# Strided v, band k and the xT ring of an attention-plus-feed-forward kernel: longer load runs with on-chip copies, and one tile fewer per ring

## The chip, the cores and the metric

The kernel runs on one core of a Trainium2 chip. The time is the device time of one launch in microseconds, as the median of several runs; most runs of the kernel before agree within some 0.3%. A run over 1.5% above the fastest of its kernel counts as slow and stays out of the ratios. HBM is the memory from which the loads read, SBUF the core's own memory, and PSUM, in banks, what matmuls write. Engine names in the profile: PE is TensorE's matmuls, PEld its weight loads, DVE VectorE, ACT ScalarE, POOL GpSimd, SP SyncE. The program fixes the order of each engine's instructions, and an engine that waits for one stands with all that come behind it, as PE will be seen to for 7.3 us; that matters more here than anything else.

## The reference, cut to what matters

```python
# q, k, v: 8 batches x 8 heads x 576 tokens x 64, fp32 in HBM
scores = (1 / sqrt(64)) * q @ k.T
mask_local   = (rel >= 0) & (rel < 32)              # heads 0..3: a band
mask_strided = (rel >= 0) & (pos_k % 32 == pos_q % 32)   # heads 4..7
attn = softmax(where(mask, scores, -1e9)) @ v
x = attn.transpose(0, 2, 1, 3).reshape(4608, 512)
h = maximum(x @ w_in, 0)                            # 512 -> 2048
out = (s * (h * h) + b) @ w_out                     # 2048 -> 512
```

The feed-forward part is called F1 (x @ w_in) and F2 (@ w_out). The loads turn fp32 into fp16, so a run that this text gives in bytes of an fp16 tile is twice as long in HBM. Attention is done in pairs of heads, four pairs to a batch (0 and 1 in the band, 2 and 3 strided), and its small matmuls are interleaved with those of F1 and F2.

## The kernel before: the parts that the change and the argument touch

The order of instructions isn't written by hand. While the program is built, a `Plan` keeps a clock for each engine, takes the next matmul step that its clock calls ready, and puts each helper copy on the engine on which it would end first by listed prices. The engines afterwards execute what came out, in that order, whatever the real times are.

```python
def flush(self):
    ...
    eng = min(p[1], key=lambda e: max(self.free[e], r) + p[1][e])
    end = max(self.free[eng], r) + p[1][eng]
    self.free[eng] = end
    p[2](eng)
```

The copy that pairs the heads of q or k (96 x 768, into a tile called qp or kp; batches 0 and 1 do without it) may go to ACT, to DVE or, in batches 1 to 3, to POOL. The issue of a whole batch's loads is also POOL's work:

```python
plan.post([key], {"A": 810, "V": 350, **({"P": 900.0} if b in (1, 2, 3) else {})}, g, ...)
...
plan.post(..., {"P": 0.0}, lambda eng, b=b: fetch_qk(b + 2), [("fetch", b + 2)])
plan.post([("fetch", b + 2)] + both("vs", b), {"P": 0.0}, lambda eng: fetch_v(b + 2), ...)
```

A third copy, the spread of a transposed q, may also go to POOL at a price of 2000, in late batches. The attention output (kind "a") of batch 0 takes its PSUM banks in rotation from a list:

```python
if b == 0:
    banks = {"a": [f2, f2, f1], "t": [t, a], "s": [("s", SB), ("s", SB), f1]}[kind]
```

Strided v of batches 0 to 3 comes as one load per batch (`vs`, 1 KB rows) and is copied on chip into `v_str`, of which there are two; batches 4 to 7 come as four loads straight into `v_str`, in short runs of one row of 64 elements (256 bytes in HBM), because `v_str` has a column of ones behind each row:

```python
def load_vs(b):
    vs = v_str[b % NV]
    for h in range(4):
        nc.gpsimd.dma_start(out=vs[:, h, :, 0:D],
                            in_=v[b, 4 + h].rearrange("(p j) d -> p j d", j=ST))
```

The softmax here doesn't subtract the row's maximum and nothing guards it: scores larger than these inputs give would overflow.

## Time and profile before

| before | value | how to read it |
|---|---|---|
| median time | 312.08 us | of 3 runs, 311.35 to 312.26; 311.72 in the 4 runs beside the changed kernel |
| span of the profiled run | 309.0 us | the profile's own clock; the launch time is about 2 us more |
| PE / DVE / ACT / POOL busy | 97% / 71% / 58% / 32% | a busy PE can hide waits; the others are far from full |
| packets of the software queue | 57,200 | the loads that POOL issues |

Two rows of slices, each a fortieth of the span (7.7 us), digits in tenths: POOL and the clock granted to PE.

```profile
POOL 8562559934951592059202950000000000000000
PEclk9999999999999999999999999999999999999999
```

POOL has work until about 185 us. The clock is full everywhere.

### The profile page before, as it was taken

What the parts mean: (1) busy time and instruction counts of PE and PEld (TensorE: products, weight loads), DVE (VectorE), ACT (ScalarE), POOL (GpSimd) and SP (SyncE); (2) the same over time, 40 slices, a digit from 0 to 9 for tenths busy, and PEclk for the clock granted to TensorE, in tenths of its full rate; (3) what the DMA queues carried; (4) which work ended last, traced back from release to release, by engine and by line L of the source; (5) the groups of instructions that cost most, each with busy time, mean ns of one, the idle gap of its engine ahead of it and who ended that gap; (6) DMA issues with size and microseconds to landing.
All of it is one profiled execution on the core that took longest, in us unless ns stands there. A gap on an engine that the chain in (4) does not pass through costs nothing.

```text
span 309.0 us, 6715 instructions
## 1 busy us (share of the span) xinstructions
PE 300.5 (97%) x2526; PEld 194.4 (63%) x2526; DVE 218.2 (71%) x575; ACT 178.3 (58%) x336; POOL 99.8 (32%) x146
## 2 busy tenths in 40 slices
PE   8899999989999999999999999999999999999994
PEld 3765655555656655556687755565677666766883
DVE  7567958799976877859755874589866366737653
ACT  1876945769736964668055736694945445356300
POOL 8562559934951592059202950000000000000000
PEclk9999999999999999999999999999999999999999
DMA  7999999998999699679998999842010100200313
GB/s 127 204 212 205 216 175 159 219 135 122 99 165 176 86 147 155 110 110 183 150 174 153 128 146 159 172 92 88 2 36 34 68 2 34 104 1 0 105 67 106
DMA packets 99940, 37.28 MB, mean 121 GB/s; under 512 B 81170, under 2 KB 95890, under 8 KB 99906
## 3 DMA queue, kind: packets, MB, share of 16 engines
q0 software_dynamic: 57200, 18.08, 60.9%
q1 hardware_dynamic: 42706, 18.76, 29.9%
q8 instruction: 20, 0.33, 0.5%
q14 instruction: 14, 0.11, 0.1%
HBM read 36.84 MB, written 10.32 MB: 153 GB/s over the span
## 4 chain that ended last, share of the span: by engine, by line
PE 82%; DMA 9%; DVE 4%; issue 2%; ACT 1%; POOL 1%; SPq 0%; DVEq 0%; POOLq 0%; ACTq 0%
PE ps_f L877 35%; PE ps_f L926 20%; PE ps_f L845 12%; DMA ql<-in_q_dram 6%; PE ps_s L531 4%; PE ps_a L585 2%; DMA w_out_sb<-in_v_dram 2%; PE ps_s L845 2%; PE ps_t L585 1%; PE ps_t L845 1%; PE ps_s L926 1%; PE ps_t L411 1%; DMA out_dram<-o 1%; PE ps_t L633 1%; DVE gT L908 1%
## 5 line engine op out<-in xcount | busy, mean ns | idle before, releaser
L877 PE MATMUL ps_f<-xT,w_in_sb 128*128 128x512 f16 (+1 forms) x632 | 148.0, 357 | 0.0
L899 ACT ACTIVATE u<-ps_f 128x512 f16<-128x512 f32 x137 | 81.1, 596 | 72.8 <-PE ps_f L877 69.5
L877 PEld LDWEIGHTS <-w_in_sb 128*128 128x128 f16 x640 | 68.1, 113 | 34.5
L926 PE MATMUL ps_f<-w_out_sb,gT 128*128 128x512 f16 x304 | 80.7, 379 | 0.2 <-DVE gT L908 0.2
L908 DVE TENSOR_TENSOR gT<-u 128x512 f16<-128x512 f16 x111 | 48.1, 438 | 31.7 <-ACT u L899 30.6
L926 PEld LDWEIGHTS <-gT 128*128 128x128 f16 x320 | 28.9, 98 | 23.2 <-DVE gT L908 0.5
L845 PEld LDWEIGHTS <-gT 128*128 128x128 f16 x320 | 31.0, 98 | 8.7
L845 PE MATMUL ps_f<-w_out_sb,gT 128*128 128x256 f16 x184 | 25.9, 273 | 0.0
L611 DVE TENSOR_TENSOR x_nat<-ps_a,rec 72x256 f16<-72x256 f32 (+1 forms) x52 | 23.7, 456 | 0.6
L547 ACT ACTIVATE p_loc<-ps_s 128x384 f16<-128x384 f32 x46 | 21.1, 493 | 5.1 <-PE ps_s L531 4.8
L547 ACT ACTIVATE p_str<-ps_s 72x432 f16<-72x432 f32 (+1 forms) x46 | 21.0, 485 | 3.2 <-PE ps_s L531 2.9
L585 PEld LDWEIGHTS <-p_str 72*128 72x128 f16 x256 | 15.5, 98 | 11.2 <-issue 1.4
L906 ACT ACTIVATE gT<-u 128x512 f16<-128x512 f16 x33 | 20.8, 630 | 1.0
L293 POOL DMA_DIRECT2D v_loc<-in_v_dram x28 | 20.6, 764 | 1.8 <-DVE qD_loc L315 1.8
L937 DVE SCALAR_TENSOR_TENSOR o<-ps_f,s_sb,bcs 128x512 f32<-128x512 f32 x19 | 14.1, 747 | 9.4 <-PE ps_f L926 9.2
L298 POOL DMA_DIRECT2D v_str<-in_v_dram x16 | 13.0, 815 | 10.7 <-PE ps_a L585 3.7
L555 DVE TENSOR_TENSOR p_str<-p_str,mask_str 72x432 f16<-72x432 f16 (+1 forms) x42 | 14.7, 360 | 1.3 <-ACT p_str L547 1.0
L555 DVE TENSOR_TENSOR p_loc<-p_loc,mask_loc 128x384 f16<-128x384 f16 x42 | 14.6, 360 | 1.2 <-ACT p_loc L547 0.9
L845 PEld LDWEIGHTS <-S 128*128 128x128 f16 x128 | 12.5, 98 | 3.2
L315 ACT COPY xT<-ps_t 128x576 f16<-128x576 f16 x9 | 5.7, 637 | 13.4 <-PE ps_t L633 13.4
L600 DVE RECIPROCAL rec<-ps_a 72x4 f32<-72x4 f32 (+1 forms) x52 | 9.1, 176 | 6.1 <-PE ps_a L585 5.5
L585 PEld LDWEIGHTS <-p_loc 128*128 128x128 f16 x192 | 10.1, 98 | 5.2 <-issue 0.7
(158 smaller groups left out, 406.4 us busy)
## 6 DMA issues: line engine op xcount, KB each, us to landing
out_dram<-o SPq DMA_DIRECT2D x34, 256.0 KB, 3.1
w_out_sb<-in_moe_w_out_dram POOLq DMA_DIRECT2D x4, 512.0 KB, 11.1
v_loc<-in_v_dram POOLq DMA_DIRECT2D x28, 72.0 KB, 7.8
ql<-in_q_dram POOLq DMA_DIRECT2D x6, 288.0 KB, 6.4
qs<-in_q_dram POOLq DMA_DIRECT2D x6, 288.0 KB, 6.2
ks<-in_k_dram POOLq DMA_DIRECT2D x6, 288.0 KB, 7.6
kl<-in_k_dram POOLq DMA_DIRECT2D x4, 288.0 KB, 8.9
kl<-in_k_dram POOLq DMA_DIRECT2D x16, 72.0 KB, 3.9
```

Source lines behind the costliest of these rows:

```text
L293: nc.gpsimd.dma_start(out=vl[LPAD:128, h, :, 0:D], in_=v_band(b, h))
L547: nc.scalar.activation(out=pt[0:nk, 0:2 * n].rearrange("k t c -> k (t c)"), in_=st["s", g][0:nk, 0:2 * n * nq], func=AF.Exp, scale=scale)
L555: nc.vector.tensor_tensor(out=pt[0:nk, 0:2 * n], in0=pt[0:nk, 0:2 * n], in1=mask, op=ALU.mult)
L585: nc.tensor.matmul(out=st["a"][:, j % per, :], lhsT=st["pw", g][0:nk, i * nq:i * nq + WIDE], rhs=vt[0:nk, 2 * mm + e, j, :])
L611: nc.vector.tensor_tensor(out=st["x"][:, j0:j0 + per, 64 * e:64 * e + 64], in0=st["pa", e, j][0:nq, 0:per, 0:D], in1=st["rec", e, j][0:nq, ...
L845: nc.tensor.matmul(out=gts[name, T, t][:, 0] if halves else gts[name, T][:, t], lhsT=lhs(k, t), rhs=rhs(k), start=fresh and k == 0 and (ha ...
L877: nc.tensor.matmul(out=gts["h", T, ft][:, lo:hi], lhsT=w_in_sb[min(ft // 4, 2)][:, ct].rearrange("p (c x l) -> p c l x", x=128, l=4)[:, ma ...
L899: nc.scalar.activation(out=gts["u", T, ft], in_=gts["h", T, ft], func=AF.Relu)
L906: nc.scalar.activation(out=gts[T][:, ft, :], in_=u, func=AF.Square)
L908: nc.vector.tensor_tensor(out=gts[T][:, ft, :], in0=u, in1=u, op=ALU.mult)
L926: nc.tensor.matmul(out=gts[id_], lhsT=gts[T][:, ft, ts * 128:(ts + 1) * 128], rhs=w_out_sb[:, ft, cols], start=(ft == 0), stop=(ft == NFT ...
L937: nc.vector.scalar_tensor_tensor(out=o[:, 0:n], in0=gts[id_], scalar=s_sb[:, 0:1], in1=bcs[:, cols], op0=ALU.mult, op1=ALU.add)
```

## The change

Its intent: fewer and longer runs in HBM. Strided v of all batches is loaded in 1 KB rows (2 KB in HBM) and copied on chip; k of the band heads of batches 4 to 7 is loaded in 768-byte runs (1.5 KB in HBM), paired by a copy, transposed by DMA and spread by another copy. SBUF for this is won by a single `v_str`, a single `vs`, and a ring of three instead of four batches in xT. The core of the diff:

```diff
-    v_str = [const.tile([SQ, 4, ST, D + 1], FP16, name=f"v_str{i}") for i in range(NV)]
+    v_str = const.tile([SQ, 4, ST, D + 1], FP16)
...
-    NX = 4
+    NX = 3
...
-            if b >= (QB_DMA if name == "q" else KB_DMA):
+            if name == "q" and b >= QB_DMA:
...
-    def load_vs(b):            # (four loads a batch, removed with its use for b >= 4)
...
-        plan.post([key], {"A": 810, "V": 350, **({"P": 900.0} if b in (1, 2, 3) else {})}, g,
+        plan.post([key], {"A": 810, "V": 350, **({"P": 900.0} if b in (1, 2, 3) or name == "k" else {})}, g,
...
+        free = [("a", (b - 1, 2 + mm), 1, ST - 1)] if b and not loc else []
-        plan.post([key], {"P": 1000.0} if loc else {"A": 2 * (170 + 0.83 * n), "V": 540.0}, g,
+        plan.post([key] + free, {"P": 1000.0} if loc else {"A": 2 * (170 + 0.83 * n), "V": 890.0}, g,
...
-            banks = {"a": [f2, f2, f1], "t": [t, a], "s": [("s", SB), ("s", SB), f1]}[kind]
+            banks = {"a": [f2, f2, f1 if m < 3 else a], "t": [t, a], "s": [("s", SB), ("s", SB), f1]}[kind]
...
+        def k_spread(eng):
+            st["k"] = kT_loc[mm]
+            copy_on(eng, out=st["k"][:, LPAD:LPAD + S].rearrange("d (p j) -> d p j", j=nt),
+                    in_=loaded[b, "kTl"][:, mm].rearrange("d j p -> d p j"))
+        if k_by_dma and loc:
+            plan.post([("in", "kl", b, mm)], {"D": 1300.0}, k_dma, [("kTl", id_)])
+            plan.post([("kTl", id_), ("s", (b - 1, m), 2)], {"V": 757.0, "A": 660.0}, k_spread, [("k", id_)])
...
-        loaded[b, "vs"] = inp.tile([SQ, NS], FP16, tag="vs", name="vs")
+        loaded[b, "vs"] = inp.tile([SQ, NS], FP16, tag="vs", bufs=1, name="vs")
```

Cut: the pair buffers go from 3 to 5, some tiles change pools, and one latency that the plan assumes for DMA transposes before 110 us goes from 5.5 to 12 us. The line on `banks` concerns one attention pair of batch 0. The changed kernel needs it: without it the plan, with its single `v_str`, stops with no step left that could become ready.

## The prediction

> **What bounds the kernel now.** I began with the page, to see which engine is full and what the chain that ended last consists of.
>
> ```profile
> PE 300.5 (97%) x2526; PEld 194.4 (63%) x2526; DVE 218.2 (71%) x575; ACT 178.3 (58%) x336; POOL 99.8 (32%) x146
> ...
> PE   8899999989999999999999999999999999999994
> ...
> DMA  7999999998999699679998999842010100200313
> ...
> q0 software_dynamic: 57200, 18.08, 60.9%
> ...
> PE 82%; DMA 9%; DVE 4%; issue 2%; ACT 1%; POOL 1%; SPq 0%; DVEq 0%; POOLq 0%; ACTq 0%
> ```
>
> The DMA row is nearly full to about 210 us, which makes it look like a transfer problem. But 82% of the chain is PE. A busy PE can hide waits, so I took the time per matmul from the chain, where runs of one kind follow each other without a gap:
>
> ```profile
> 146.48 3.02 PE ps_f L926 x14
> ...
> 236.53 4.04 PE ps_f L845 x37
> ```
>
> 3.02/14 is 0.216 us for a matmul of 512 columns, 4.04/37 is 0.109 for 256. In the same way the chain gives 0.083 for 192 columns, 0.063 for 144, 0.055 for 128, 0.043 for 96, 0.033 for 65 and 72, and 0.023 and 0.063 for two kinds that run beside each other (paired transposes of the first batches, sums over w_out). Multiplied by the counts of the program, in its order, this is the PE stream: 293.6 us in all, of which 5.1 are filler matmuls of the start. The last matmul ends near 304.5, then an eviction and a store take the rest of the 309.0 us. So PE stands still for about 11 us, and where is decisive. The first transpose of batch 1's q starts at 29.10 us, at 21.9 us of the stream: 7.2 us of the idle time lie before it, in the start, which waits for first loads. From 29.10 to 304.5 the clock advances 275.4 us and the stream 271.65, so only 3.75 us are left there. The chain shows most of those in one place:
>
> ```profile
> 60.45 0.19 DVE rec L600
> 60.65 1.65 DVE v_str L315 x4
> 62.30 0.46 DVE x_nat L611
> 62.76 0.06 DVE gT L908
> 62.82 0.78 issue
> ```
>
> That is four copies of strided v in a row on DVE, holding back an attention eviction. The table by stretches says how full the helpers are there and later (columns: stretch, length, then busy us and instructions of PE, PEld, DVE, ACT, POOL, then clock, DMA share, GB/s):
>
> ```profile
> 95.00:210.00 115.00, 115.00 (x919) 71.80 (x918) 82.62 (x252) 72.90 (x141) 40.79 (x61) 1.00 1.33 142
> 57.00:77.00 20.00, 18.74 (x177) 11.27 (x175) 18.57 (x43) 16.66 (x33) 10.54 (x16) 1.00 1.07 165
> ```
>
> DVE is 93% busy from 57 to 77 us, but 72% from 95 to 210, with ACT at 63%. After 95 us the chain is PE alone: late batches, which this change is about, keep no PE waiting. The waits seen there belong to others:
>
> ```profile
> ACT u L899 <- PE ps_f L877: 69.5, 77, 6.7
> POOL gate L997 <- DMA kT<-ks: 35.0, 6, 16.4
> ```
>
> ACT stood idle 69.5 us for matmuls, and POOL 35.0 for a transpose before loading a batch two ahead; both are slack.
>
> **What the Trainium skill says.** "Perfetto Trace Analysis", section "Identifying the Most-Contended Engine": matmul busy time doesn't show how near the limit a kernel is, since matmuls are pipelined. The trace agrees: busy counts 379 ns for a matmul that advances the chain by 216, hence the stream above. "DMA: Bandwidth & Descriptors", section "Why small descriptors are slow (HBM only)": each packet of a short HBM transfer pays a fixed overhead, 27% for one of 256 bytes. That is the length of the source runs which the change replaces. The trace fits without proving it: the software queue moves 18.08 MB in 60.9% of the engines' time, and the hardware queue 18.76 MB in 29.9%. "SBUF — State Buffer", section "Who interferes with whom": VectorE and GpSimd share a pair of ports, and a VectorE instruction with two SBUF inputs contends with a GpSimd one that reads SBUF. The trace agrees: of these two rows the second has gT products at 0.8 us each, where their median is about 0.41:
>
> ```profile
> 72.11 3.03 POOL L315 COPY qD_str<-qT 64x576 f16<-64x576 f16 x4 [7.76 <-DMA qT<-qs]
> 72.27 1.59 DVE L908 TENSOR_TENSOR gT<-u 128x512 f16<-128x512 f16 x2
> ```
>
> **The change part by part.** *Strided v, batches 4 to 7.* A batch's four loads of 72x8 runs become one of 72x4: 2304 runs to 288. Issues on POOL: 12 fewer at 0.81 us, 9.8 us. Added are 16 copies of 72x512, at 0.29 to 0.40 us on DVE or 0.62 on ACT. In the built program the copies rise from 6 to 20 on ACT and from 10 to 12 on DVE: 14x0.62 = 8.7 us of ACT, 0.8 of DVE. DVE's share in the crowded early stretch falls, because the plan prices a pair at 890 instead of 540. v_str becomes single, so a batch's copy also waits for the previous batch's last use.
>
> *Band k, batches 4 to 7.* 2304 runs to 384 a batch; 12 fewer issues at 0.75 us, 9.0 us of POOL. Added: 8 pairing copies (in the build 2 more on ACT at 0.83, 2 on DVE at 0.35, 4 on POOL at 0.93) and 8 spreads of 128x576: 5 on ACT at about 0.64, 3 on DVE at perhaps 0.4. The DMA transposes stay 8. Together with v, ACT gains 13.6 us in the late stretch (63% to 75%), DVE about 3 (72% to 75%), and 4x0.93 of POOL copies disturb DVE less than their own length. POOL loses some 19 us of issuing. About 15,700 runs leave the software queue of 57,200 packets. All of it lies beside PE: value on the path, 0.
>
> *Ring of three.* xT of batch b may be written one F1 tile or more later. In both built orders I compared the last reader's place with the next need: for batch 6 the write is free at 169 us of the stream and F1 of tile 6 begins at 204; for batch 7 it is free at 200, needed at 230. A transpose of x lands in 9.3 us, so nothing waits. The wrap cuts two tiles instead of one, 64 matmuls more, with the same columns: 0.1 us.
>
> *The order that results.* The change also alters planned latencies, so the whole order is made anew. Stream after: 294.4 us, of which 5.8 filler. Up to q of batch 1 it has the same length (21.95), but 0.7 of useful work was displaced by filler; what is left behind 29.1 us is 272.4, +0.8. Next, in before 6 F1 matmuls (1.3 us) stand between transposes of q and k of batch 1, and PE still waited a little for k at 31.15; after has 3 (0.65), with k's and q's strided transposes directly behind one another. Those loads do not land sooner, so PE should wait 0.7 us for k and some 0.2 for strided q: +0.9. In exchange part of the jam at 60 to 66 us goes: -0.6. For copies on ACT or DVE that now and then stand ahead of an eviction in order, I allow +0.4.
>
> Sum: 0.8 + 0.9 - 0.6 + 0.4 = +1.5. The launch time follows the span, so 312.1 + 1.5, rounded down a little because late waits may absorb some of the start's: 313.4 us.
>
> **The rivals.** *The transfers are the limit after all*, and short runs cost several per cent: for it, the full DMA row; against it, the chain after 95 us and ACT's wait for PE. It would give 300 to 306. *DVE and ACT become the bound*: copies of 1.2 us in pairs on ACT ahead of the relu that frees one of two F1 banks. For it: F1's four matmuls take only 0.86 us. Against: 75% load, and the plan interleaves F2 and attention. It would cost 0.3 us a time, up to 5 in all: 316 to 319. *The longer path of k* (load, pairing, transpose, spread) comes late and PE stalls in order: against it, the plan allows 12 us for a transpose that lands in 2.8 to 9.3; for it, two copies sit on POOL behind a wait for another transpose. One late batch costs 2 to 5 us: 315 to 318. *A pure gain at the crowded stretch*, with no waits in the start: 310.
>
> **Range and chances.** The path offers at most 3.75 us behind the start, so faster by 2% (under 305.8) needs the start to shrink as well, and its loads are unchanged: 0.02. Slower by 2% (over 318.3) needs two rivals at once, or one badly: 0.07. Within 2%: 0.91. Eight in ten: 310.5 to 316.8.
>
> **What would show it.** Right: packets of the software queue near 41,000 and its share well below 60.9%; POOL busy near 85; ACT near 190; chain after 95 us still PE; the first q transpose still near 29.1, and a wait for k of batch 1 just behind it; the four-in-a-row v copies gone from the chain. Wrong: v_str, kT_loc or kTl named as releasers of PE for over 1 us in sum after 95 us; PE waiting for xT; a PE gap in late slices; or an end below 308, which would mean that transfers did hold PE in a way this chain doesn't show.

## The result, and the profile after

The changed kernel took 325.85 us (median of 4 runs, 323.69 to 329.22) beside 311.72 for the kernel before (4 runs, 311.12 to 312.26). It is slower by 4.3%: the ratio is 1.043, with an interval of 1.034 to 1.053. Ratios here are the mean time of one kernel's fast runs over that of the other's from the same rounds, so not quite the ratio of the medians quoted. One of the four runs, 329.22, counted as slow and is left out of it. The three fast ones still lie 4 us apart, where those of the kernel before lie within 1.1; why is not known. All runs gave right results.

The page of the changed kernel: busy times, the rows of slices, the software queue and the chain that ended last.

```profile
PE 305.3 (95%) x2593; PEld 199.3 (62%) x2593; DVE 223.6 (69%) x586; ACT 189.5 (59%) x351; POOL 83.6 (26%) x122
...
PE   8898994699999999999999999999999999999995
...
PEclk9999799599999999999999999999999999999999
...
q0 software_dynamic: 38384, 18.07, 46.7%
...
PE 77%; DMA 11%; POOL 4%; issue 3%; DVE 2%; SPq 1%; ACT 1%; POOLq 0%; DVEq 0%; ACTq 0%
```

The loads did what they were meant to: a third fewer packets, their share of the DMA engines down from 60.9% to 46.7% for the same 18 MB (58.6 to 62.5% in the four traces with 57,200 packets, 46.7 to 53.5% in the eight with 38,384). The time is lost elsewhere, and the PE row says where: the seventh and eighth digits, 4 and 6, are a hole of some 7 us around 55 us. The clock row has a 5 right behind it, and a 7 near 36 us. That is in batches 1 and 2, whose loads the change leaves as they were.

I read the waits next (columns: engine and line, what it waited for; us in total, times, the longest).

```profile
POOL vs L288 <- ACT v_str L308: 26.4, 3, 10.7
...
PE ps_t L405 <- POOL qp L308: 7.3, 1, 7.3
```

PE waited once, for 7.3 us, for qp, the paired q of batch 2, copied by POOL. The other line, POOL's 26.4 us for the copies into `v_str` before it may issue a load of `vs`, becomes important later. Here is PE around the hole, with start, length, engine, line, operation and, in brackets, what it waited for:

```profile
51.23 0.40 PE L954 MATMUL ps_s<-w_out_sb,w_mix 128*32 128x512 f16 x4
58.93 0.66 PE L405 MATMUL ps_t<-ident,qp 96*128 96x96 f16 x6 [7.30 <-POOL qp L308]
```

And POOL in the same stretch of the changed kernel. The first line issues the strided v of batch 2; the six behind it load q and k of batch 3, for which no step of batch 2 needs to wait:

```profile
50.33 0.73 POOL L288 DMA_DIRECT2D vs<-in_v_dram  x1 [0.21 <-issue]
51.06 0.67 POOL L273 DMA_DIRECT2D ql<-in_q_dram  x1
51.72 0.67 POOL L273 DMA_DIRECT2D kl<-in_k_dram  x1
52.38 1.80 POOL L282 MEMSET qs<- 16x2048 f16 x1
54.48 0.72 POOL L288 DMA_DIRECT2D qs<-in_q_dram  x1 [0.30 <-POOL qs L282]
55.19 1.80 POOL L282 MEMSET ks<- 16x2048 f16 x1
57.28 0.72 POOL L288 DMA_DIRECT2D ks<-in_k_dram  x1 [0.30 <-POOL ks L282]
58.05 0.82 POOL L308 COPY qp<-ql 96x768 f16<-96x768 f16 x1
```

Without a gap to speak of, five issues of about 0.7 us and two memsets of 1.80 us stand ahead of the copy. The data had landed long before: ACT copied the other pair of the same tile at 50.5 us. The plan had none of these issues on its clock: it charges 0 for them. The surprise is in the kernel before, where POOL did the same thing at nearly the same time. First POOL's copy of a batch 2 pair there, then the transposes of PE that use it, then DVE's copy of the other pair:

```profile
57.31 0.82 POOL L315 COPY qp<-ql 96x768 f16<-96x768 f16 x1
```

```profile
58.47 0.41 PE L411 MATMUL ps_t<-ident,qp 96*128 96x96 f16 x6
```

```profile
48.26 0.31 DVE L315 COPY qp<-ql 96x768 f16<-96x768 f16 x1
```

In both kernels one qp copy of batch 2 lands on POOL at the end of this burst. Before, it was that of the *second* pair, done at 58.13, and PE asked for it at 58.47, so it was in time by 0.34 us; the first pair's had been done by DVE at 48.57. In the changed kernel POOL has the *first* pair's, which PE wants as soon as the matmuls placed ahead of it are done, at 51.63. The changed order did not make POOL slower; it gave POOL's late slot to an operand that is needed some 7 us sooner.

The table by stretches shows the cost behind the wait too (stretch, length, then busy us and instructions of PE, PEld, DVE, ACT and POOL; then granted clock, DMA share, GB/s). After:

```profile
32.00:36.00 4.00, 3.51 (x47) 2.80 (x47) 2.17 (x5) 2.92 (x6) 3.05 (x5) 0.59 1.15 218
...
51.00:59.00 8.00, 0.70 (x11) 0.34 (x10) 0.78 (x3) 0.95 (x2) 7.36 (x9) 0.85 1.53 168
59.00:64.00 5.00, 5.00 (x37) 2.95 (x38) 1.49 (x6) 1.61 (x3) 3.53 (x5) 0.56 1.39 139
```

Before:

```profile
51.00:59.00 8.00, 8.00 (x84) 4.86 (x83) 5.97 (x16) 4.00 (x8) 7.36 (x9) 1.00 1.33 179
59.00:64.00 5.00, 4.72 (x46) 2.75 (x45) 4.61 (x12) 3.79 (x8) 5.00 (x7) 1.00 1.39 227
```

POOL is busy 7.36 us of the 8 in both; PE is busy 8.00 in one and 0.70 in the other. From 59 to 64 us PE is busy all the time, yet executes 37 matmuls at a clock of 0.56. The Trainium skill, "TensorE: Matmul & The Clock Gate", section "What's actually happening", says that the clock halves after at least one idle window of about 3.4 us and comes back after a busy one. The traces agree in length: the slow stretches of the changed kernel last 3.4 us (32.7 to 36.1) and 6.8 us (56.6 to 63.4), one window and two. They don't agree that the window before must be wholly idle; the last section comes back to this. In a slow stretch a matmul takes about twice as long, so the first one costs 1.7 us, and the second, in which PE stood until 58.93, about 2 us.

**The account.** As in the prediction, I multiplied the matmul durations by the counts of the program to get the time for which PE's stream needs a full clock, and took the rest as standing still, or as slow clock. (A wait counted in this way, between the starts of matmuls, comes out 0.1 to 0.2 us longer than in the brackets above, which count from the end that the profile models.) For the start of the last matmul:

| term | before | after | difference |
|---|---|---|---|
| PE's stream at full clock | 293.87 | 294.70 | +0.83 |
| standing, 0 to 15 us | 4.05 | 4.03 | 0.0 |
| standing, 15 to 45 us (first loads, q and k of batch 1) | 2.73 | 4.45 | +1.7 |
| standing, 45 to 60 us (qp of batch 2) | 0.70 | 7.63 | +6.9 |
| standing, 60 to 90 us (the jam on DVE) | 1.98 | 0.85 | -1.1 |
| standing, after 90 us | 0.05 | 1.79 | +1.7 |
| half clock | 0 | 3.57 | +3.6 |
| start of the last matmul | 304.4 | 318.1 | +13.7 |

Each column is about 1 us short of its last row, because the first matmul starts at 1.05 or 1.07 us. The differences add up within rounding to 13.6. The spans of these two traces differ by 12.9 us, since what follows the last matmul is 0.8 us shorter in the changed kernel. The largest single wait after 90 us is one of 0.72 us that ends at 152.1. POOL's timeline ahead of it, and PE's matmuls behind it:

```profile
141.76 2.89 POOL L270 DMA_DIRECT2D ql<-in_q_dram  x4 [0.31 <-issue]
...
149.73 0.73 POOL L288 DMA_DIRECT2D vs<-in_v_dram  x1
150.46 1.56 POOL L308 COPY qD_str<-qT 64x576 f16<-64x576 f16 x2
...
152.07 0.35 PE ps_s L530 x3
```

It is the same pattern: POOL issues the loads of a late batch from 141.76 to 150.46 us, and the spread of a q that PE soon stands for comes behind them.

### The profile page after: what moved, and what is told of

Same layout as the page of the kernel before. It is cut to its first block, busy times and chain, and to the rows that moved or that the text cites.

```text
span 321.9 us, 6836 instructions
## 1 busy us (share of the span) xinstructions
PE 305.3 (95%) x2593; PEld 199.3 (62%) x2593; DVE 223.6 (69%) x586; ACT 189.5 (59%) x351; POOL 83.6 (26%) x122
## 3 DMA queue, kind: packets, MB, share of 16 engines
q0 software_dynamic: 38384, 18.07, 46.7%
## 4 chain that ended last, share of the span: by engine, by line
PE 77%; DMA 11%; POOL 4%; issue 3%; DVE 2%; SPq 1%; ACT 1%; POOLq 0%; DVEq 0%; ACTq 0%
PE ps_f L878 32%; PE ps_f L927 19%; PE ps_f L846 12%; DMA ql<-in_q_dram 6%; PE ps_s L530 4%; DMA kl<-in_k_dram 2%; PE ps_a L584 2%; DMA w_out_sb<-in_v_dram 2%; PE ps_s L846 2%; PE ps_t L405 1%; PE ps_t L846 1%; PE ps_s L927 1%; PE ps_t L584 1%; DMA kT<-ks 1%; POOL ql L270 1%
## 5 line engine op out<-in xcount | busy, mean ns | idle before, releaser
L878 PE MATMUL ps_f<-xT,w_in_sb 128*128 128x512 f16 (+4 forms) x696 | 148.8, 341 | 0.0
L878 PEld LDWEIGHTS <-w_in_sb 128*128 128x128 f16 x704 | 70.6, 113 | 33.5 <-issue 0.9
L927 PE MATMUL ps_f<-w_out_sb,gT 128*128 128x512 f16 x304 | 82.1, 385 | 0.2 <-DVE gT L909 0.2
L909 DVE TENSOR_TENSOR gT<-u 128x512 f16<-128x512 f16 x115 | 51.7, 456 | 27.4 <-ACT u L900 26.0
L293 POOL DMA_DIRECT2D v_loc<-in_v_dram x28 | 20.6, 743 | 2.1 <-DMA kl<-in_k_dram 1.3
L907 ACT ACTIVATE gT<-u 128x512 f16<-128x512 f16 x29 | 18.3, 630 | 0.9
L530 PE MATMUL ps_s<-qD_loc,kT_loc 128*128 128x192 f16 x92 | 14.7, 251 | 0.0
L308 ACT COPY v_str<-vs 72x512 f16<-72x512 f16 x20 | 11.5, 620 | 5.5 <-PE ps_a L584 3.4
L554 DVE TENSOR_TENSOR p_str<-p_str,mask_str 72x432 f16<-72x432 f16 (+1 forms) x42 | 14.0, 341 | 0.7 <-ACT p_str L546 0.5
L288 POOL DMA_DIRECT2D vs<-in_v_dram x10 | 6.8, 684 | 27.7 <-ACT v_str L308 26.4
```

Of the source, the lines that this page charges most:

```text
L293: nc.gpsimd.dma_start(out=vl[LPAD:128, h, :, 0:D], in_=v_band(b, h))
L530: nc.tensor.matmul(out=st["s", g][0:nk, c:c + 2 * nq], lhsT=(st["k"][:, i * nq:i * nq + nk] if loc else st["k"][:, i, 0:SQ]), rhs=st["q"][ ...
L554: nc.vector.tensor_tensor(out=pt[0:nk, 0:2 * n], in0=pt[0:nk, 0:2 * n], in1=mask, op=ALU.mult)
L878: nc.tensor.matmul(out=gts["h", T, ft][:, lo:hi], lhsT=w_in_sb[min(ft // 4, 2)][:, ct].rearrange("p (c x l) -> p c l x", x=128, l=4)[:, ma ...
L907: nc.scalar.activation(out=gts[T][:, ft, :], in_=u, func=AF.Square)
L909: nc.vector.tensor_tensor(out=gts[T][:, ft, :], in0=u, in1=u, op=ALU.mult)
```

## The experiments

Two theories stood at first. **A**: one line of the diff, the bank choice of batch 0, changes the built order; batch 2's first q goes to POOL behind load issues; that wait and the slow clock behind it are most of the loss. **B**: the loss comes from the headline parts (longer path of k, single `v_str`, more copies on ACT and DVE), and the hole is only where it shows. A third was added later: with POOL's copies gone, the single `v_str` is what remains. Each edit of a price or a buffer makes the built order anew, so a rival to A is that the edit helped by another order of PE. The traces speak against it: PE's recorded matmuls have one and the same order in the changed kernel and in experiments 2, 3, 4 and 9 up to the 512th, and the one that waits is the 506th; it starts at 58.93 us in the changed kernel and at 50.5 to 53.4 in these four. Experiments 1 and 5 agree in the same way up to the 534th; the one that waits starts at 59.59 and at 49.99. The ratios are those to the kernel before in the same rounds; its medians there were 312.19, 311.78, 311.78 and 311.63 us (experiments 1 to 4; 5 to 8; 9 to 11; 12).

### 1. The bank line alone

The kernel before, with this one line of the change:

```diff
-            banks = {"a": [f2, f2, f1], ...}
+            banks = {"a": [f2, f2, f1 if m < 3 else a], ...}
```

> The kernel before with one line of the change alone: the fourth head pair of batch 0 takes its attention bank from another pool. No load, no copy, no buffer of the headline parts is touched, but the built order flips: the pairing copy of batch 2's first q pair moves from DVE to POOL, and PE wants it at 41.2 us of its stream. Theory A (the loss is PE standing in order behind a copy that POOL reaches only after its queue of load issues): PE stalls 5 to 8 us near 52 us, the clock halves after it, time 319 to 324. Rival B (the headline parts cost it: longer path of k, single v_str, ring of three, more copies on ACT): as before, 310 to 313.

Measured: 322.16 us, ratio 1.032 (1.029 to 1.035). No load was changed, and 10 of the 14 us are there. The chain of waits around the hole:

```profile
55.86 1.81 POOL ks L282
...
58.71 0.83 POOL qp L315
...
59.59 0.66 PE ps_t L411 x6
```

The memset for batch 3's k, POOL's copy, and PE's transposes as soon as it ends: the same chain as in the changed kernel. PE had stood 9.3 us between starts, a little more than I expected (5 to 8), and the clock was halved from 53.2 to 63.4 us, three windows long. Theory A holds for the early loss.

### 2. No pairing copy of batch 2 on POOL, in the changed kernel

```diff
-{"P": 900.0} if b in (1, 2, 3) or name == "k"
+{"P": 900.0} if b in (1, 3) or name == "k"
```

> The changed kernel, but batch 2's q pairs may not be paired on POOL. The order then puts the first k pair of batch 2 on POOL, wanted at 44.5 us of the stream instead of 40.3. Theory A: the stall does not vanish but shrinks by about those 4.2 us, to about 3 us, with at most a short half clock: 317 to 321. Rival B: no change, 324 to 328. If the first q pair alone were the trouble, whatever waits behind it: 314 or less.

Measured: 321.80 us (320.53 to 324.35), ratio 1.032. Only q of batch 2 leaves POOL by this edit; its k may still go there, by the second half of the condition. The hole shrank from about 7.5 to 2.7 us, now before kp, as expected, but the time fell by 4 us only, just outside the 317 to 321 that I had written. A new wait of 2.58 us came late. The chain there:

```profile
171.69 20.57 DMA v_loc<-in_v_dram
...
192.34 0.04 ACT v_loc L308
...
192.98 0.59 ACT u L900
...
193.60 3.19 PE ps_f L878 x8
```

The band v of batch 7 landed 20.6 us after its issue, a copy of it stood in ACT's order ahead of a relu, and PE waited for the relu. The 8 matmuls of the last line take 3.19 us, 0.40 each instead of 0.216: half clock again (194.0 to 197.4 us). So a late wait took back a part of what was removed early. That is no proof of B, but it showed that the early hole isn't all.

### 3. No pairing copy on POOL at all, in the changed kernel

```diff
-{"A": 810, "V": 350, **({"P": 900.0} if b in (1, 2, 3) or name == "k" else {})}
+{"A": 810, "V": 350}
```

> The changed kernel, pairing copies on ACT or DVE only. Theory A: the 7.6 us stall and its half clock (together some 10 us) go; what stays is the wait for batch 1's k near 32 us and the late POOL wait for a q spread: 313 to 317. Rival B: 322 to 328, since all headline parts are still there and ACT and DVE are fuller still.

Measured: 318.22 us (317.28 to 323.25), ratio 1.019 (1.015 to 1.022), a little above what I expected. The early hole is gone; there are new waits of 1.53 us at 141.4 and of 4.05 us at 174.8 us. POOL's timeline before the latter:

```profile
169.70 2.92 POOL L293 DMA_DIRECT2D v_loc<-in_v_dram  x4
172.60 0.74 POOL L288 DMA_DIRECT2D vs<-in_v_dram  x1
173.33 1.40 POOL L308 COPY qD_str<-qT 64x576 f16<-64x576 f16 x2
```

PE stands until the second copy ends. These are the spreads of q, the one kind of copy that is left on POOL, and again they stand behind load issues.

### 4. No copy on POOL, in the changed kernel

As 3, and the spreads too:

```diff
-            plan.post([("qT", id_), ...], {"P": 2000.0, "V": 940.0, "A": 1340.0}, q_spread,
+            plan.post([("qT", id_), ...], {"V": 940.0, "A": 1340.0}, q_spread,
```

> As the run before, and the spreads of strided q are kept off POOL too, so POOL only issues loads. Theory A: another 0.7 to 1.5 us less than that run, from the wait near 152 us: 312 to 316. Rival B: 322 to 328, or slower than the changed kernel because ACT and DVE carry more.

Measured: 316.02 us (314.62 to 319.60), ratio 1.011 (1.007 to 1.014), at the upper edge of what theory A expected. 10 us of 14 are gone, and 4 remain with no copy on POOL. In the profiled run (316.70 us) the clock was halved from 32.7 to 39.5 us behind the waits for batch 1, which is about 3 us of its loss; the fastest run, 314.62, had a mean clock of 1.00. Its chain late in the kernel:

```profile
178.83 15.55 DMA vs<-in_v_dram
...
194.41 0.90 DVE v_str L308 x4
```

The strided v of batch 7 lands late, and its copies hold up DVE, behind which PE waits 0.72 us until 199.1. A wait of 1.42 us that ends at 191.7 is for a relu on ACT, behind a copy of the band v of the same batch, which lands late too.

### 5. The bank line, and no copy on POOL, in the kernel before

Experiment 1 with the two edits of experiment 4.

> The kernel before with the bank line of the first run, but pairing copies and q spreads kept off POOL. If the bank line lost its 3% only through a copy standing behind POOL's load issues (theory A), the loss goes: 311 to 314, no PE gap over 1 us between 45 and 60 us. If the other bank itself costs (attention evictions of batch 0 waiting for one bank), it stays: 318 to 323.

Measured: 310.83 us (310.18 to 311.70, 20 runs), ratio 0.997 (0.996 to 0.998). The bank line costs nothing once POOL has no copy to be late with. This is the sharpest pair: experiments 1 and 5 share the line, and differ by 11 us. It has the lowest median of all kernels that were run, 0.3% below the kernel before; of this, experiment 8 finds 0.15% without the bank line, and the rest was not followed up.

### 6. Strided v alone, 7. band k and ring alone, in the kernel before

Each on the kernel before, with two `v_str` kept and without the bank line.

```diff
-    LONG_V = 4                      # experiment 6
+    LONG_V = 8
```

> The kernel before with the first headline part alone: strided v of batches 4 to 7 in 1 KB rows with the copy, all buffers and banks as before. The order of the first 80 us is the same as before. Theory A (headline parts lie beside the path): 310 to 314, software queue packets down by about 8,000, its share down by some 7 points, and no gain from it. Rival B: 315 to 320 from ACT copies ahead of evictions. Rival C (transfers bound it): below 307.

```diff
-    NX = 4                          # experiment 7, with the k hunks of the change
+    NX = 3                          # and four pair buffers instead of three
```

> The kernel before with the two other headline parts: band k of batches 4 to 7 in 768-byte runs, paired, transposed by DMA and spread, and the ring of three (which makes the room). Bank, strided v and the order of the first 80 us as before. Theory A: 310.5 to 315; a late pairing copy or two still falls to POOL, which may cost PE 1 to 2 us at one batch. Rival B: 316 to 322, with PE waiting for kT_loc or xT.

Measured: 312.22 us for v, ratio 1.001 (1.000 to 1.003), with 46,256 packets in the software queue; and 312.30 us for k and the ring, ratio 1.003 (1.001 to 1.004), with 49,328 packets. Both times are within their ranges. The packets of v are not: 10,944 fewer, where about 8,000 were expected. The queue's share is 52.6% with v alone and 59.7% with k alone, and the latter lies inside the scatter of unchanged loads (58.6 to 62.5%): the relief of the DMA engines comes from v. Of what the change is named after, neither part was measured to cost or gain more than 0.3%. Theory B in its main form fell here.

### 8. The kernel before without copies on POOL

The two edits of experiment 4 on the kernel before.

> The kernel before, with pairing copies and q spreads kept off POOL. Theory A: even there POOL copies bring little and slow DVE through the shared port at 60 to 76 us; 308.5 to 312, a candidate to beat both. If they relieve DVE more than they cost: 312 to 315.

Measured: 311.04 us, ratio 0.998 (0.997 to 1.000). The kernel before loses next to nothing by its POOL copies. So POOL's copies are harmless here and cost about 10 us in experiment 1, by which operand they carry and when PE needs it, not by their number (qp and kp are copied there twice each in the kernel before).

### 9. Only batch 2 off POOL, in the changed kernel

```diff
-**({"P": 900.0} if b in (1, 2, 3) or name == "k" else {})
+**({"P": 900.0} if b != 2 and (b == 3 or name == "k") else {})
```

> The changed kernel, with the pairing copies of batch 2 alone kept off POOL (q and k), all later ones as the plan likes. Theory A: the one stall near 52 us and its half clock go, some 10 us, and the late POOL waits stay: 314.5 to 318. If the several late waits made the loss together, and not this one: 320 or more.

Measured: 314.87 us (313.45 to 316.57), ratio 1.010 (1.006 to 1.013). All other batches may still use POOL (q of batch 1, which the edit also bars, is never paired), yet 11 us are gone. It goes further than experiment 2, because k of batch 2 leaves POOL as well, and it ends no slower than experiment 4, where no copy is left on POOL: of all copies there, the ones of this single batch carry nearly all of the loss. The late wait for a q spread stays: 1.86 us, at 142.6.

### 10. Filler matmuls in the wait

How much of the loss is the slow clock? The changed kernel, with 31 matmuls of no use put ahead of the transposes that wait for qp, into the bank that these overwrite:

```diff
+                    if (b, m, name) == (2, 0, "q"):
+                        for _ in range(31):
+                            nc.tensor.matmul(out=bank(group), lhsT=ones16,
+                                rhs=ones16[:, None, :].to_broadcast([128, 4, 128]), start=True, stop=True)
```

> The changed kernel, in the same order, with 31 filler matmuls (6.7 us) put where PE stands still for the copy of batch 2's first q pair. The wait is as long as before, but PE is busy in it. If the half clock after the stall comes from PE's idling, it does not fall in that stretch, and the time drops by 2 to 3 us, to about 323; if the low clock has another cause (it would then be there without idling), no change: 325 to 328.

Measured: 326.12 us (6 runs, two of them slow), ratio 1.041 (1.036 to 1.046). The changed kernel's own ratio is 1.043 (1.034 to 1.053), so no gain is shown; with intervals this wide, one of 2 to 3 us isn't excluded either. The windows of this run:

```profile
51.00:59.00 8.00, 6.33 (x30) 2.65 (x28) 0.00 (x0) 0.17 (x1) 6.50 (x7) 1.00 1.48 167
59.00:64.00 5.00, 4.79 (x57) 3.01 (x58) 2.76 (x10) 2.59 (x4) 3.83 (x6) 1.00 1.25 126
```

The clock stayed at 1.00, and PE executed 57 matmuls from 59 to 64 us where the changed kernel executed 37. So the slow clock behind the hole does come from PE's idling, as was thought; the mean clocks of the fast runs agree, 0.995 to 0.999 here and 0.977 to 0.984 in the changed kernel. The stretch from 32 to 36 us isn't settled by this: its clock is full here too, though nothing was added there and PE stood as long from 15 to 45 us, some 4.4. The 2 to 3 us that I expected don't show in the time, because PE stood longer elsewhere in the profiled run, some 4.4 us after 90 us instead of 1.8: the wait before the spread at 151 us is 1.56 us here instead of 0.72, and there is one of 1.93 us at 201.7. That PE came sooner to operands that did not come sooner is my reading of it, not shown. This was a miss: the half clock's 3.6 us in the account are real time in which PE was slow, but removing most of it did not measurably shorten the kernel.

### 11. All headline loads, with two `v_str`, and 12. the same with one

Both are the changed kernel without copies on POOL and with four pair buffers instead of five, so that two `v_str` fit; they differ in `v_str` alone.

```diff
-    v_str = const.tile([SQ, 4, ST, D + 1], FP16)          # 12 keeps this
+    v_str = [const.tile([SQ, 4, ST, D + 1], FP16, name=f"v_str{i}") for i in range(NV)]
...
-        free = [("a", (b - 1, 2 + mm), 1, ST - 1)] if b and not loc else []
+        free = [("a", (b - 2, 2 + mm), 1, ST - 1)] if b > 1 and not loc else []
```

> All headline parts (strided v with its copy, band k with pairing and spread, ring of three) and the bank line, no copies on POOL, but v_str doubled again (room from one pairing buffer less). It differs from the run without POOL copies (316.0) in the single v_str. If the rest of the loss, 3.8 us, is the order that the single v_str forces (waits for first loads of batch 1, late copies of batch 7), this is 310.5 to 313. If the longer paths of k and v cost it, 315 to 317.

> The last run with one v_str instead of two, and nothing else changed (all headline loads, bank line, no copies on POOL, four pairing buffers). If the single v_str is what the rest of the loss hangs on (its copy waits for the previous batch's last use, the load of the next batch's strided v waits for the copy, and POOL's later loads stand behind that load): 314.5 to 317.5, POOL waiting over 10 us before one strided v load. If the fifth pairing buffer or chance of the half clock made the difference: 311 to 313.5.

Measured: 312.02 us with two (22 runs, two of them slow), ratio 1.002 (1.000 to 1.003); 316.46 us with one (315.68 to 317.70), ratio 1.017 (1.014 to 1.019). Both within their ranges. A single `v_str` costs 4.4 us between the medians, and everything else in the change, with POOL kept free, about 0.2. How it costs: the load of `vs` for the same batch on POOL in experiment 12 (timeline, in brackets what POOL waited for),

```profile
122.48 0.73 POOL L288 DMA_DIRECT2D vs<-in_v_dram  x1 [13.58 <-ACT v_str L308]
```

and in experiment 11:

```profile
110.36 0.73 POOL L288 DMA_DIRECT2D vs<-in_v_dram  x1 [0.48 <-DVE rec L599]
```

With one `v_str`, the copies of a batch wait for the previous batch's last use of it; `vs`, also single, is free only after the copies; and POOL, in order, stands 13.6 us at 122 us for that. After 90 us PE stands 4.7 us in experiment 12 and 0.4 in experiment 11, which is about the whole difference. Its two large waits, 1.93 and 1.64 us between starts:

```profile
185.87 1.24 PE L878 MATMUL ps_f<-xT,w_in_sb 128*128 128x512 f16 x5 [1.76 <-DMA xT<-x_dram]
...
198.08 0.24 PE L584 MATMUL ps_t<-v_loc,p_loc 128*128 128x65 f16 x2 [1.48 <-DVE p_loc L554]
```

The second stands behind DVE's copies of batch 7's strided v, which was issued 2.2 us later than in experiment 11 and took 18.3 us to land instead of 12.3. The first is for a transpose of x, which took 11.6 us to land instead of 3.6 (medians from 160 to 200 us). So transfers that land late are what PE pays for. That they land late because POOL stood at 122 us is likely, but the links between were not followed: POOL begins batch 7's loads only 0.6 us later. With two, the chain that ended last is PE alone:

```profile
PE 87%; DVE 0%; issue 0%
```

### All of them

| kernel | us | ratio |
|---|---|---|
| changed kernel | 325.85 | 1.043 |
| 1 bank line alone | 322.16 | 1.032 |
| 2 changed, q of batch 2 off POOL | 321.80 | 1.032 |
| 3 changed, no pairing on POOL | 318.22 | 1.019 |
| 4 changed, no copies on POOL | 316.02 | 1.011 |
| 9 changed, batch 2 off POOL | 314.87 | 1.010 |
| 10 changed, filler in the wait | 326.12 | 1.041 |
| 12 as 4, four pair buffers | 316.46 | 1.017 |
| 11 as 12, two v_str | 312.02 | 1.002 |
| 6 before, strided v | 312.22 | 1.001 |
| 7 before, band k and ring | 312.30 | 1.003 |
| 8 before, no copies on POOL | 311.04 | 0.998 |
| 5 before, bank line, no copies on POOL | 310.83 | 0.997 |

So the loss splits, by the ratios, which leave slow runs out, times 311.7 us: 13.4 us in all, 0.5 for the loads themselves (11), 4.6 for the single `v_str` (12 against 11), and 8.3 for copies on POOL (the changed kernel against 12), the last uncertain by some 3 us. Differences of medians give 14.1 as 0.2, 4.4 and 9.4. The last step also takes away a fifth pair buffer; experiment 4, which keeps it, is at 1.011 (1.007 to 1.015) beside 1.017 (1.014 to 1.019) of 12, so that copies on POOL alone may be worth 10 us. Nothing here beats the kernel before by 2%. What is left open: how the part of POOL's copies divides into the wait and the slow clock, since experiment 10 took most of the slow clock away without a gain that shows; how a single `v_str` makes the transfers of batch 7 late; and why the bank line without POOL copies gains 0.3%.

## Why the prediction was wrong

**That PE bounds the kernel and the transfers are hidden: right.** The software queue's share fell by 14 points and bought nothing; experiments 6, 7 and 11 are within 0.3% of before. The rival that transfers are the limit is gone. POOL came out as worked out (83.6 for "near 85"), and the value of the parts on the path, 0, was right for v, k and the loads. The packets did not quite: 38,384 for "near 41,000", with 10,944 fewer for v where 8,064 runs were counted. ACT's 189.5 for "near 190" is partly luck: the spreads of k took 1.19 us on ACT and 0.65 on DVE instead of 0.64 and 0.4, and other work must have fallen away. (The DMA row, read as nearly full to 210 us, is so to about 200.)

**The ring of three: no cost seen.** Experiment 7 has it with band k at +0.5 us, and experiment 11 with everything else at +0.2. Experiment 12 does have a wait of 1.76 us for xT, for a transpose that landed late; that the ring held it back is not seen, and experiment 11, with the same ring, has no such wait.

**The terms of the sum.** Stream +0.8: measured +0.83. The waits for k and strided q behind batch 1's first q, +0.9: +0.9 from 30 to 45 us (1.13 us before k alone). But that first q, held to stay at 29.1 us, started at 30.05, another +0.8. The jam, -0.6: -1.1, and its four copies are gone from the chain. Helpers in the late stretch, +0.4: +1.7; the chain after 95 us is mostly PE as predicted, except for the part from 134 to 152 us shown above. These give +3.2 instead of +1.5: too low by 1.7 us even without the rest.

**The step that failed is "The order that results".** It says that "the whole order is made anew", and then follows the new order to batch 1's q and k and takes the rest as the old one with a jam less. Nothing in it asks what else was rearranged. What was missing, 6.9 us of wait for qp of batch 2 and about 2 of half clock behind it, stands at 51 to 63 us, beyond where the comparison ended; the other 1.7 of half clock, at 32.7 to 36.1 us, follow waits that were foreseen, whose effect on the clock was not. All that was needed was known: the order of the changed kernel's build shows a q copy of batch 2 move to POOL ahead of the first pair's transposes, and the trace of before shows POOL reach that slot at 57.31, while PE wants the copy at 40.3 us of its stream (the figure in the expectation of experiment 2). By the prediction's own 29.1 us for 21.95 of the stream that is about 48 on the clock, an estimate; in the trace it was 51.6. Either is many us before POOL's copy. The prediction looked for a danger on POOL only in late k, as a rival at 2 to 5 us.

**The single `v_str` was named and not priced.** The change part says that "a batch's copy also waits for the previous batch's last use", and stops there. The next two links, that `vs` is single too and that POOL issues in order, turn this into POOL standing up to 13.6 us (experiment 12), and experiments 11 and 12 put 4.4 us to it. The rival on k had the right form (a late operand, PE stalled in order, 2 to 5 us for one late batch), but on another tensor.

**The chances** gave 0.07 to slower, for "two rivals at once, or one badly". A rebuilt order is a third way, and it needed no rival.

**The checks that the prediction set for itself did not catch this.** Most of its signs of being right came true, and none of its signs of error did: it looked for "a PE gap in late slices", and the gap came in early ones.

## What to carry to other kernels

Where a program's order is computed from prices, a change of one buffer can move any copy to any engine, so compare the whole built order before predicting, operand by operand, and place each moved copy at the time at which the old trace shows its new engine reach that slot. An engine that issues loads in order is a bad place for a copy that another engine stands for: POOL looked 32% busy, and its copy still came 7 us late, because its work comes in bursts that the plan prices at 0. And halving a buffer can cost along the whole queue that waits for it (4.4 us here): ask who issues the refill, and what else stands behind that issue.

## What the Trainium skill lacked or had wrong

- "Perfetto Trace Analysis", section "DMA Instruction — SWDGE (GPSIMD)", says that the profiled interval of such a load is the time in which GpSimd generates descriptors. It gives no length. Here an issue keeps POOL for about 0.7 us (0.67 to 0.73 ahead of the late copy), and a copy or memset behind it waits: 7 us for five issues and two memsets of 1.80 us (16x2048, fp16). No page that I read warns against putting a copy that TensorE needs behind them.
- "GPSIMD Engine Reference", section "4.1 Engine selection", calls one-input work on GpSimd roughly line-rate, in a row that advises between GpSimd and VectorE. That must not be read as VectorE's rate: the pairing copy, 96x768 in fp16, took 0.82 us on POOL and 0.31 us on DVE in the kernel before (0.34 to 0.59 in experiments 1 and 5), up to 2.6 times as long.
- "TensorE: Matmul & The Clock Gate", section "What's actually happening", has the clock halve after at least one idle window of about 3.4 us. The changed kernel's first slow stretch, 3.4 us from 32.7, followed waits of only about 1 us each (0.92 and 1.13); in the 3.4 us before it, 29.3 to 32.7, the profile has PE busy half of the time. A wholly idle window wasn't needed. Nor does half always suffice: from 49.8 to 53.2, two such windows before the next slow stretch, PE was busy 54% and the clock stayed full.
- "DMA: Bandwidth & Descriptors", section "Why small descriptors are slow (HBM only)", gives a fixed overhead for each packet and no measure of what longer runs buy inside a kernel. Here the effect is there for v (share of the software queue 52.6% instead of 60.9%, with 256-byte runs become 2 KB) and within the scatter for k (59.7%); and it buys no time, since PE does not wait for those loads (312.02 us with all of them, beside 311.78).
